# W3's last 64 features by tokens, W4 of tiles 0 to 2 with its output turned

## The chip, the core and the metric

The kernel runs on one core of one Trainium2 chip. Its engines run side by side, each with its own queue in which work is done in order: TensorE (PE in the profile; its weight loads are listed as PEld), VectorE (DVE), ScalarE (ACT), GpSimd (POOL) and SyncE (SP), which here issues almost all DMAs. The metric is the device time of one execution in microseconds (us), the median of several runs.

## The reference

The input x has 2048 tokens of 640 features. The result is a gated sum of a linear attention block and an MLP block with shifts between tokens:

```python
g = _sigmoid((x * gate_w).sum(-1, keepdims=True))
a = _A_ref(x, A_wqkv, A_wo)                 # linear attention, 32 heads of 20
b = _B_ref(x, B_w1, B_w2, B_w3, B_w4)
return g * a + (1 - g) * b

# _B_ref
h = _gelu(_layernorm(x, axis=-1) @ w1)
hs = jnp.concatenate([g0, g1, g2, g3], axis=-1) @ w2     # g0..g3: quarters of h, shifted by 1, -1, 2, -2 tokens
x1 = x + hs
h2 = _gelu(_layernorm(x1, axis=-1) @ w3) @ w4            # w3: 640 x 1728, w4: 1728 x 640
return x1 + h2
```

The change concerns w3 and w4. The inner width 1728 is 13 blocks of 128 features and a rest of 64.

## The kernel before, in words

The tokens are handled in four tiles of 512 (`TS`), each of four chunks of 128 (`CPT`). A first part, up to line 425, loads everything, makes the keys, queries and the attention's small matrix, and W1 of tiles 0 and 1. The part that the change touches is the loop over tiles at the end (L599 to L616). The order of the work on every engine is the order in which the program is written out (`tc.manual_schedule()`); nothing reorders it.

For a tile `t` the loop runs seven W3 units (`w3_unit`, L474). A unit does two blocks of 128 features (the last one does one): the weights of W3 are the stationary operand, the tile's 512 normalized tokens `lnT` are moved through, and the result, features on partitions and tokens in columns, goes through a gelu on ScalarE (L485) into `h2`. Between the units stand chunks of other work. `w2_unit` (L429) makes `x1` for a later tile and its statistics on VectorE (L439, L293 to L295), `ln2_apply` (L449) normalizes it (L453) and has it turned by a DMA transpose on SP. Tile 0 does this for tile 1, and tile 1 for tiles 2 and 3 (`ahead`, L598), so unit 2 and unit 3 of tile 1 are each followed by two W2 chunks. `att_unit` (L462) computes the attention's output of one chunk of tile `t` and VectorE adds it, times the gate, into `x1` (L470); its four chunks follow units 2 to 5.

The last 64 features of W3 (`w3_rest`, L488) are computed for two tiles at a time: after tile 0's units for tiles 0 and 1, in tile 1's W4 for tiles 2 and 3. The weights have 64 columns, so the left and the right half of the array work at once on the two halves of the tokens.

W4 (`w4_tile`, L548) takes a chunk of 128 tokens of `h2` as the stationary operand and moves w4's 640 output features through, as 256 and 384 columns. The result has tokens on partitions and features in columns, like the output. A chunk's 13 blocks are summed in PSUM; the 64 features of the rest are added by `w4_rest` (L521), in which upper and lower half of the array's rows work at once for two chunks. VectorE then forms `omg * result + x1` for all 640 features (L532), where `omg` is 1 - g and `x1` has been scaled by `omg` on ScalarE (`x1_scale`, L457), and SP stores the chunk (L537). `scale_t` (L276) scales the queries of the next tile on VectorE.

PSUM is handed out in pairs of two banks, four pairs in all:

```python
ps = ctx.enter_context(tc.tile_pool(name="ps", bufs=4, space=PSUM))
def pair():
    return ps.tile([P, 2, 512], F32, name="pp")
```

A new pair waits for the readers of an earlier one. The output chunks have two buffers (`outp`), and `hx_p` has two buffers of 512 columns, used by W1's last block (L359).

Of the kernel before, what the change touches and what calls it, by code (L numbers as in the profile page):

```python
# [7 lines left out]
ACT = mybir.ActivationFunctionType  # L8
ALU = mybir.AluOpType
BF16 = mybir.dt.bfloat16  # L10
# [6 lines left out]
def kernel(  # L17
# [13 lines left out]
    nc = tc.nc  # L31
    P = 128
    S, D = A_x.shape[1], A_x.shape[2]
    F = B_w3.shape[1]
    H, Dh = 32, 20
    NCH = S // P
    TS = 512
    NT = S // TS
    CPT = TS // P
    DC = D // P  # L40
    HD = D // 2
    FF = F // P
    FR = F - FF * P
# [12 lines left out]
    out2 = out.rearrange("b s d -> (b s) d")  # L56
# [4 lines left out]
    const = ctx.enter_context(tc.tile_pool(name="const", bufs=1))  # L61
    small = ctx.enter_context(tc.tile_pool(name="small", bufs=4))
    work = ctx.enter_context(tc.tile_pool(name="work", bufs=4))
    hx_p = ctx.enter_context(tc.tile_pool(name="hx_p", bufs=2))
    outp = ctx.enter_context(tc.tile_pool(name="outp", bufs=2))
    lnx_p = ctx.enter_context(tc.tile_pool(name="lnx_p", bufs=3))
    ps = ctx.enter_context(tc.tile_pool(name="ps", bufs=4, space=PSUM))
# [3 lines left out]
    def pair():  # L71
        return ps.tile([P, 2, 512], F32, name="pp")
# [4 lines left out]
    pqT = const.tile([P, DC, S], BF16)  # L77
# [3 lines left out]
    w3_sb = const.tile([P, DC, F], BF16)  # L81
# [16 lines left out]
    omg = const.tile([P, NCH], F32)  # L98
# [133 lines left out]
    for c in range(2, NCH):  # L232
        pt = pair()
# [42 lines left out]
    def scale_t(t):  # L276
        sl = pqT[:, :, t * TS:(t + 1) * TS]
        nc.vector.tensor_tensor(sl, sl, rb[:, t:t + 1, :].broadcast_to([P, DC, TS]), op=ALU.mult)
# [130 lines left out]
    w4_sb = w4p.tile([P, FF + 1, D], BF16)  # L409
    h2x_p = ctx.enter_context(tc.tile_pool(name="h2x_p", bufs=2))  # L410
# [15 lines left out]
    st = {}  # L426
# [17 lines left out]
    def ln2_rstd(t, c0, c1):  # L444
        if c0 == 0:
            st[t]["rstd"] = small.tile([P, CPT], F32, name="rstd2")
        rsqrt(st[t]["rstd"][:, c0:c1], st[t]["mv"][:, c0:c1, 1])
# [9 lines left out]
    def x1_scale(t, cc):  # L457
        c = t * CPT + cc
        x1 = st[t]["x1"][cc]
        nc.scalar.activation(x1[:], x1[:], ACT.Copy, scale=omg[:, c:c + 1])  # L460

    def att_unit(t, cc):  # L462
        c = t * CPT + cc
        pt = pair()
        for hf in range(2):
            for j in range(DC):
                nc.tensor.matmul(pt[:, hf, 0:HD], lhsT=pqT[:, j, c * P:(c + 1) * P],  # L467
                                 rhs=m_sb[:, j, hf * HD:(hf + 1) * HD], start=(j == 0), stop=(j == DC - 1))
        x1 = st[t]["x1"][cc][:].rearrange("p (h e) -> p h e", h=2)
        nc.vector.scalar_tensor_tensor(x1, pt[:, :, 0:HD], gate[:, c:c + 1], x1, op0=ALU.mult, op1=ALU.add)  # L470

    LT = TS // 2

    def w3_unit(t, i):  # L474
        if i == 0:
            st[t]["h2"] = h2p.tile([P, FF * TS], BF16, name="h2")
        h2, lnT = st[t]["h2"], st[t]["lnT"]
        pt = pair()
        n = min(2, FF - 2 * i)
        for k in range(n):  # L480
            fc = 2 * i + k
            for dc in range(DC):
                nc.tensor.matmul(pt[:, k, :], lhsT=w3_sb[:, dc, fc * P:(fc + 1) * P], rhs=lnT[:, dc, :],  # L483
                                 start=(dc == 0), stop=(dc == DC - 1))
        nc.scalar.activation(h2[:, 2 * i * TS:(2 * i + n) * TS], pt[:].rearrange("p h e -> p (h e)")[:, 0:n * TS],  # L485
                             ACT.Gelu_apprx_tanh)

    def w3_rest(ts, dsts):  # L488
        for t, dst in zip(ts, dsts):
            for dc in range(DC):  # L490
                for v in range(2):
                    nc.tensor.matmul(dst[FR * v:FR * (v + 1), :], lhsT=w3_sb[:, dc, FF * P:F],  # L492
                                     rhs=st[t]["lnT"][:, dc, v * LT:(v + 1) * LT], start=(dc == 0), stop=(dc == DC - 1))
        for t, dst in zip(ts, dsts):
            st[t]["h2x"] = h2x_p.tile([P, LT], BF16, name="h2x")
            nc.scalar.activation(st[t]["h2x"][:], dst, ACT.Gelu_apprx_tanh)

    NW = D - TS

    def w4_tiles(t, ccs, pts):  # L500
        if t < NT - 1:
            for cc in ccs:
                pt = pair()
                pts[cc, 0], pts[cc, 1] = (pt[:, 0, TS - LT:TS], 0, LT), (pt[:, 1, 0:D - LT], LT, D)
                pts[cc, "rest"] = pt[:, 0, 0:LT]
                pts[cc] = pt[:].rearrange("p h e -> p (h e)")[:, TS - LT:TS - LT + D]
        else:
            for _ in range(3 if 0 in ccs else 1):
                pts["pairs"] = pts.get("pairs", []) + [pair()]
            homes = {0: (0, 1), 2: (1, 2)} if 0 in ccs else {1: (3, 3), 3: (2, 0)}  # L510
            for cc, (w, n) in homes.items():
                wide, narrow = pts["pairs"][w][:, 0, :], pts["pairs"][n][:, 1, 0:NW]
                pts[cc, 0], pts[cc, 1] = (narrow, 0, NW), (wide, NW, D)

    def w4_mm(t, cc, pts, hf, start):
        dst, a, b = pts[cc, hf]
        for fc in range(FF):
            nc.tensor.matmul(dst, lhsT=st[t]["h2"][:, fc * TS + cc * P:fc * TS + (cc + 1) * P],  # L518
                             rhs=w4_sb[:, fc, a:b], start=start and fc == 0, stop=not start and fc == FF - 1)

    def w4_rest(t, pts):  # L521
        for u in range(2):
            for hf in range(2):
                for v in range(2):
                    rows = slice(FR * v, FR * (v + 1))
                    dst, a, b = pts[u + 2 * v, hf]
                    nc.tensor.matmul(dst, lhsT=st[t]["h2x"][rows, u * P:(u + 1) * P],  # L527
                                     rhs=w4_sb[rows, FF, a:b], start=u == 1, stop=u == 0)

    def w4_stt(t, cc, oc, src, a, b):  # L530
        c = t * CPT + cc
        nc.vector.scalar_tensor_tensor(oc[:, a:b], src, omg[:, c:c + 1], st[t]["x1"][cc][:, a:b],  # L532
                                       op0=ALU.mult, op1=ALU.add)

    def w4_store(t, cc, oc, a, b):
        c = t * CPT + cc
        nc.sync.dma_start(out2[c * P:(c + 1) * P, a:b], oc[:, a:b])  # L537

    def w4_out(t, cc, pts):
        oc = outp.tile([P, D], BF16, name="oc")  # L540
        if t < NT - 1:
            w4_stt(t, cc, oc, pts[cc], 0, D)
        else:
            for hf in range(2):
                w4_stt(t, cc, oc, *pts[cc, hf])
        w4_store(t, cc, oc, 0, D)

    def w4_tile(t):  # L548
        last = t == NT - 1
        pts = {}  # L550
        if not last:
            scale_t(t + 1)
        w4_tiles(t, (0, 2), pts)
        for cc in (0, 2):
            if not last:
                x1_scale(t + 1, cc)
            for hf in (1, 0):
                w4_mm(t, cc, pts, hf, True)
        w4_tiles(t, (1, 3), pts)
        w4_rest(t, pts)  # L560
        if t == 1:
            w3_rest((2, 3), (pts[0, "rest"], pts[2, "rest"]))
        for cc in (0, 2):
            w4_out(t, cc, pts)
        ocs = {}
        for cc, hf in ((1, 1), (3, 1), (1, 0), (3, 0)) if last else ((1, 0), (1, 1), (3, 0), (3, 1)):
            if not last and hf == 0:
                x1_scale(t + 1, cc)
            w4_mm(t, cc, pts, hf, False)
            if last:  # L570
                if hf == 1:
                    ocs[cc] = outp.tile([P, D], BF16, name="oc")
                w4_stt(t, cc, ocs[cc], *pts[cc, hf])
                w4_store(t, cc, ocs[cc], *pts[cc, hf][1:])
            elif hf == 1:
                w4_out(t, cc, pts)

    for cc in range(CPT):
        w2_unit(0, cc)
# [18 lines left out]
    ahead = {0: ((1, 0),), 1: ((2, 0), (3, 2))}  # L598
    for t in range(NT):  # L599
        for i in range(NW3):  # L600
            w3_unit(t, i)
            for u, i0 in ahead.get(t, ()):
                if 0 <= i - i0 < CPT:
                    w2_unit(u, i - i0)
                    ln2_rstd(u, i - i0, i - i0 + 1)
                    if i > i0:
                        ln2_apply(u, i - i0 - 1)
            if 2 <= i < 2 + CPT:
                att_unit(t, i - 2)
            for u, i0 in ahead.get(t, ()):  # L610
                if i - i0 == CPT - 1:
                    ln2_apply(u, CPT - 1)
        if t == 0:
            pt = pair()
            w3_rest((0, 1), (pt[:, 0, 0:LT], pt[:, 1, 0:LT]))
        w4_tile(t)  # L616


# [28 lines left out]
```

## Time and profile before

| | |
|---|---|
| three runs | 263.14, 263.43, 264.2 us; median 263.43 |
| profiled execution: span, first to last instruction | 261.2 us; what lies around it in that execution isn't recorded, and the median is 2.2 us above the span |
| TensorE busy | 257.1 us, 98% |
| VectorE, ScalarE, GpSimd busy | 141.6, 83.4, 26.9 us |
| W4 stage of tile 0 (128.36 to 143.25 us) | 14.89 us, TensorE 14.89, VectorE 2.72, ScalarE 3.52 |
| W3 stage of tile 1 (143.25 to 173.58 us) | 30.33 us, TensorE 30.33, VectorE 21.61, ScalarE 6.14 |
| granted TensorE clock in both | 1.00 |

The span is cut into 40 slices on the page, and each engine's busy share is given for a slice. The chain of work that ended last is followed back from the end of the kernel; an engine that takes nearly all of it sets the time. A line like L483 names the line of the kernel that issued the instruction. "Idle before" is the time in which an engine stood still just before an instruction, with the work that ended it.

### The profile page before, as it was taken

To read this page: it belongs to the slowest core of one execution; us is meant where nothing else is said; L and a number is where in the kernel's file an instruction comes from. 1 tells how busy PE (TensorE), PEld (TensorE's weight loads), DVE (VectorE), ACT (ScalarE), POOL (GpSimd) and SP (SyncE) were. 2 spreads that over 40 slices of the span, in tenths; PEclk is the share of its full clock that TensorE was granted. 3 is DMA by queue.
4 is the path that set the end of the run, shared out by engine and by line. 5 is a ranking of instruction groups with operands and counts; after the bars stand their busy time and mean duration, and the time that the engine had idled before them with its cause. 6 is when DMAs were issued, how large, how long until landed. Compare 5 with 4: busy or idle time off the path is not lost.

```text
span 261.2 us, 4169 instructions
## 1 busy us (share of the span) xinstructions
PE 257.1 (98%) x1669; PEld 158.7 (61%) x1669; DVE 141.6 (54%) x276; ACT 83.4 (32%) x125; POOL 26.9 (10%) x82
## 2 busy tenths in 40 slices
PE   7999999999999999999999999999999999999995
PEld 3777555788754644565676566567745567455553
DVE  2688778899947884967312378970312223112132
ACT  2655554321165446531520311140233350142100
POOL 3000050012220140131000123310000000000000
PEclk9999999999999999999999999999999999999999
DMA  7999997016684826996002011321200001100011
GB/s 210 203 138 376 365 267 318 0 28 125 125 100 86 220 56 143 173 311 83 0 3 75 25 28 25 75 54 25 77 25 0 0 3 50 53 0 0 0 53 50
DMA packets 47281, 25.78 MB, mean 99 GB/s; under 512 B 35230, under 2 KB 46494, under 8 KB 47262
## 3 DMA queue, kind: packets, MB, share of 16 engines
q1 hardware_dynamic: 46820, 25.03, 39.4%
q10 hardware_dynamic: 442, 0.49, 0.5%
q8 instruction: 13, 0.21, 0.4%
q14 instruction: 6, 0.05, 0.1%
HBM read 13.03 MB, written 3.60 MB: 64 GB/s over the span
## 4 chain that ended last, share of the span: by engine, by line
PE 97%; DMA 2%; SPq 0%; DVE 0%; issue 0%
PE pp L518 22%; PE pp L483 21%; PE pp L319 8%; PE pp L436 8%; PE pp L467 8%; PE pp L353 8%; PE pp L242 8%; PE pp L187 8%; DMA wk_sb<-in_A_wqkv_dram 2%; PE pp L527 1%; PE pp L492 1%; PE pp L386 1%; PE pp L372 1%; PE pp L257 0%; SPq L120 0%; SPq L126 0%
## 5 line engine op out<-in xcount | busy, mean ns | idle before, releaser
L483 PE MATMUL pp<-lnxT,w_sb 128*128 128x512 bf16 x260 | 60.0, 379 | 0.0
L518 PE MATMUL pp<-w_sb,h 128*128 128x384 bf16 (+3 forms) x416 | 57.9, 299 | 0.0
L485 ACT ACTIVATE h<-pp 128x1024 bf16<-128x1024 f32 (+1 forms) x28 | 26.9, 962 | 94.3 <-PE pp L483 94.3
L518 PEld LDWEIGHTS <-h 128*128 128x128 bf16 x416 | 38.3, 98 | 19.4 <-issue 1.2
L483 PEld LDWEIGHTS <-w_sb 128*128 128x128 bf16 x260 | 25.4, 98 | 27.2
L532 DVE SCALAR_TENSOR_TENSOR oc<-pp,omg,x 128x640 bf16<-128x640 f32 (+2 forms) x20 | 14.4, 748 | 45.4 <-PE pp L527 21.2
L470 DVE SCALAR_TENSOR_TENSOR x<-pp,gate,x 128x640 f32<-128x640 f32 x16 | 14.1, 879 | 33.6 <-PE pp L467 33.6
L179 ACT ACTIVATE e<-pp 128x640 bf16<-128x640 f32 (+1 forms) x26 | 21.5, 827 | 9.6 <-PE pp L242 9.6
L467 PE MATMUL pp<-m_sb,pqT 128*128 128x320 bf16 x160 | 24.3, 299 | 0.0
L436 PE MATMUL pp<-w_sb,hsT 128*128 128x320 bf16 x160 | 23.5, 299 | 0.0
L187 PE MATMUL pp<-wk_sb,xT 128*128 128x320 bf16 (+1 forms) x160 | 22.4, 300 | 0.5 <-DVE xT L216 0.3
L319 PE MATMUL pp<-x_sb,pk 128*128 128x320 bf16 (+1 forms) x160 | 22.0, 300 | 0.0
L242 PE MATMUL pp<-xT,hsT 128*128 128x512 bf16 x100 | 21.7, 379 | 0.0
L319 PEld LDWEIGHTS <-pk 128*128 128x128 bf16 x160 | 18.8, 117 | 3.2
L436 PEld LDWEIGHTS <-hsT 128*128 128x128 bf16 x160 | 15.6, 98 | 7.7
L467 PEld LDWEIGHTS <-pqT 128*128 128x128 bf16 x160 | 15.7, 98 | 7.7
L187 PEld LDWEIGHTS <-xT 128*128 128x128 bf16 x160 | 15.5, 98 | 6.9 <-DVE xT L216 0.6
L289 POOL TENSOR_SCALAR rstd<-mv 128x1 f32<-128x1 f32 (+1 forms) x20 | 7.7, 385 | 115.3 <-DVE mv L295 115.3
L439 DVE TENSOR_TENSOR x<-pp,x_sb 128x640 f32<-128x640 f32 x16 | 13.1, 818 | 10.7 <-PE pp L436 10.6
L353 PE MATMUL pp<-lnxT,w_sb 128*128 128x512 bf16 x80 | 18.1, 379 | 0.0
L242 PEld LDWEIGHTS <-hsT 128*128 128x128 bf16 x100 | 11.8, 118 | 9.7
L181 DVE SCALAR_TENSOR_TENSOR pk<-pp,e 128x640 bf16<-128x640 f32 x16 | 13.2, 825 | 1.7
(73 smaller groups left out, 190.3 us busy)
## 6 DMA issues: line engine op xcount, KB each, us to landing
x_sb<-in_A_x_dram SPq DMA_DIRECT2D x1, 2240.0 KB
out_dram<-oc SPq DMA_DIRECT2D x14, 160.0 KB, 1.8
w_sb<-in_B_w_dram SPq DMA_DIRECT2D x1, 2160.0 KB
w_sb<-in_B_w_dram SPq DMA_DIRECT2D x1, 2080.0 KB, 12.2
wo_sb<-in_A_wo_dram SPq DMA_DIRECT2D x6, 160.0 KB, 7.5
m_dram<-x SPq DMA_DIRECT2D x3, 320.0 KB, 2.8
hsT<-in_A_wqkv_dram SPq DMA_DIRECT2D x1, 800.0 KB, 5.4
m_sb<-in_A_wqkv_dram SPq DMA_DIRECT2D x1, 800.0 KB
```

Of the source, the lines that this page charges most:

```text
L179: nc.scalar.activation(ev, src, ACT.Exp)
L187: nc.tensor.matmul(pt[:, hf, 0:n], lhsT=xT[:, dc, c * P:(c + 1) * P], rhs=wk_sb[:, dc, hf * HD:hf * HD + n], start=(dc == first), stop=(dc ...
L242: nc.tensor.matmul(pt[:, t % 2, :], lhsT=wq_sb[:, dc, :].rearrange("p (m j) -> p j m", j=DC)[:, j], rhs=xT[:, dc, t * TS:(t + 1) * TS], st ...
L319: nc.tensor.matmul(pt[:, hf, 0:HD + hf], lhsT=w, rhs=x_sb[:, c, hf * HD:(hf + 1) * HD + hf], start=(c == 0), stop=(c == NCH - 1))
L353: nc.tensor.matmul(pt[:, i, :], lhsT=w, rhs=lnxT[t][:, dc, :], start=(dc == 0), stop=(dc == DC - 1))
L436: nc.tensor.matmul(pt[:, hf, 0:HD], lhsT=hsT[:, fc, 2 + c * P:2 + (c + 1) * P], rhs=w2_sb[:, fc, hf * HD:(hf + 1) * HD], start=(fc == 0), ...
L467: nc.tensor.matmul(pt[:, hf, 0:HD], lhsT=pqT[:, j, c * P:(c + 1) * P], rhs=m_sb[:, j, hf * HD:(hf + 1) * HD], start=(j == 0), stop=(j == D ...
L470: nc.vector.scalar_tensor_tensor(x1, pt[:, :, 0:HD], gate[:, c:c + 1], x1, op0=ALU.mult, op1=ALU.add)
L483: nc.tensor.matmul(pt[:, k, :], lhsT=w3_sb[:, dc, fc * P:(fc + 1) * P], rhs=lnT[:, dc, :], start=(dc == 0), stop=(dc == DC - 1))
L485: nc.scalar.activation(h2[:, 2 * i * TS:(2 * i + n) * TS], pt[:].rearrange("p h e -> p (h e)")[:, 0:n * TS], ACT.Gelu_apprx_tanh)
L518: nc.tensor.matmul(dst, lhsT=st[t]["h2"][:, fc * TS + cc * P:fc * TS + (cc + 1) * P], rhs=w4_sb[:, fc, a:b], start=start and fc == 0, stop ...
L532: nc.vector.scalar_tensor_tensor(oc[:, a:b], src, omg[:, c:c + 1], st[t]["x1"][cc][:, a:b], op0=ALU.mult, op1=ALU.add)
```

## The change

W3's last 64 features are now computed tile by tile, inside the pair of `att_unit` of chunk 0: the stationary operand is a chunk of 128 normalized tokens in the full array, the moving operand W3's last 64 columns, five matmuls for each of four chunks. The results have tokens on partitions. Two gelus write them twice, side by side, into a buffer of `hx_p`, and a DMA transpose turns that into `h2x`, features on partitions, both halves of the partitions holding the same 64 features.

W4 of tiles 0 to 2 is turned round: w4 is the stationary operand and `h2` with its 512 tokens moves through, for five blocks of 128 output features. The first four blocks have a bank each, in two pairs; the fifth is cut into two halves of 256 tokens in the two banks of a third pair. The 64 features of the rest come first. After each block ScalarE copies it to a buffer of `hx_p` (now three buffers), and a DMA transpose turns it into `pqT`, whose columns of this tile are no longer needed. The output step, with `x1`, follows in the next tile before its W3 unit 2, from SBUF. The last tile's W4 is as before, written out in one function; its rest takes the columns of `h2x` of its own chunk.

```diff
-    hx_p = ctx.enter_context(tc.tile_pool(name="hx_p", bufs=2))
+    hx_p = ctx.enter_context(tc.tile_pool(name="hx_p", bufs=3))
...
     def att_unit(t, cc):
...
+        if cc == 0:
+            w3_rest_mm(t, pt)
+            w3_rest_evac(t, pt)
         x1 = st[t]["x1"][cc][:].rearrange("p (h e) -> p h e", h=2)
         nc.vector.scalar_tensor_tensor(x1, pt[:, :, 0:HD], gate[:, c:c + 1], x1, op0=ALU.mult, op1=ALU.add)
...
-    def w3_rest(ts, dsts):
...
+    def w3_rest_mm(t, pt):
+        for u in range(2):
+            for v in range(2):
+                cc = 2 * u + v
+                for dc in range(DC):
+                    nc.tensor.matmul(pt[:, u, HD + FR * v:HD + FR * (v + 1)], lhsT=st[t]["lnT"][:, dc, cc * P:(cc + 1) * P],
+                                     rhs=w3_sb[:, dc, FF * P:F], start=(dc == 0), stop=(dc == DC - 1))
+
+    def w3_rest_evac(t, pt):
+        hr = hx_p.tile([P, TS], BF16, name="hx")
+        for r in range(2):
+            nc.scalar.activation(hr[:].rearrange("p (u v r f) -> p u v r f", u=2, v=2, r=2)[:, :, :, r],
+                                 pt[:, :, HD:HD + 2 * FR].rearrange("p u (v f) -> p u v f", v=2), ACT.Gelu_apprx_tanh)
+        st[t]["h2x"] = h2x_p.tile([P, TS], BF16, name="h2x")
+        nc.sync.dma_start_transpose(st[t]["h2x"][:].rearrange("p (c s) -> p c s", c=CPT), hr[:])
...
+    def w4_turned(t):
+        scale_t(t + 1)
+        prs = [pair() for _ in range(3)]
+        bank = [prs[d // 2][:, d % 2, :] for d in range(DC)]
+        outs = [(d, bank[d], 0, TS) for d in range(CPT)]
+        outs += [(CPT, bank[CPT][:, 0:LT], 0, LT), (CPT, prs[2][:, 1, 0:LT], LT, TS)]
+        for n, (d, dst, a, b) in enumerate(outs):
+            rows = slice(FR * (n % 2), FR * (n % 2 + 1))
+            nc.tensor.matmul(dst, lhsT=w4_sb[rows, FF, d * P:(d + 1) * P], rhs=st[t]["h2x"][rows, a:b],
+                             start=True, stop=False)
+        for d in range(DC):
+            if d < CPT:
+                x1_scale(t + 1, d)
+            for fc in range(FF):
+                for e, dst, a, b in outs:
+                    if e == d:
+                        nc.tensor.matmul(dst, lhsT=w4_sb[:, fc, d * P:(d + 1) * P],
+                                         rhs=st[t]["h2"][:, fc * TS + a:fc * TS + b], start=False, stop=(fc == FF - 1))
+            hT = hx_p.tile([P, TS], BF16, name="hx")
+            if d < CPT:
+                nc.scalar.copy(hT[:], bank[d])
+            else:
+                nc.scalar.copy(hT[:].rearrange("p (v s) -> p v s", v=2), prs[2][:, :, 0:LT])
+            nc.sync.dma_start_transpose(pqT[:, d, t * TS:(t + 1) * TS].rearrange("p (c f) -> p c f", c=CPT), hT[:])
+
+    def w4_turned_out(t, cc):
+        c = t * CPT + cc
+        oc = outp.tile([P, D], BF16, name="oc")
+        o = t * TS + cc * P
+        nc.vector.scalar_tensor_tensor(oc[:].rearrange("p (d f) -> p d f", d=DC), pqT[:, :, o:o + P], omg[:, c:c + 1],
+                                       st[t]["x1"][cc][:].rearrange("p (d f) -> p d f", d=DC), op0=ALU.mult, op1=ALU.add)
+        nc.sync.dma_start(out2[c * P:(c + 1) * P, :], oc[:])
...
-    def w4_tile(t):
...
+    def w4_last(t):
...
     for t in range(NT):
         for i in range(NW3):
+            if t > 0 and i == 2:
+                for cc in range(CPT):
+                    w4_turned_out(t - 1, cc)
             w3_unit(t, i)
...
-        if t == 0:
-            pt = pair()
-            w3_rest((0, 1), (pt[:, 0, 0:LT], pt[:, 1, 0:LT]))
-        w4_tile(t)
+        if t < NT - 1:
+            w4_turned(t)
+        else:
+            w4_last(t)
```

In the changed file the gelus of the rest are line L502, the remainder matmuls of the turned W4 L517, its main matmuls L525, the copies L529 and L531, their transposes L532, and the output step L538.

More of the change, by code (lines that the diff above doesn't have):

```diff
@@ L486, in w3_unit @@
                              ACT.Gelu_apprx_tanh)
-    def w3_rest(ts, dsts):
[L489 to L496, printed above, removed]
@@ L498 @@
-    NW = D - TS
-    def w4_tiles(t, ccs, pts):
-        if t < NT - 1:
-            for cc in ccs:
-                pt = pair()
[L504 to L528, printed above, removed]
+    def w3_rest_mm(t, pt):
[5 more added lines that the diff above has]
+                                     rhs=w3_sb[:, dc, FF * P:F], start=(dc == 0), stop=(dc == DC - 1))
@@ L537, in w4_store, with place, mm @@
         nc.sync.dma_start(out2[c * P:(c + 1) * P, a:b], oc[:, a:b])
[L539 to L543, printed above, removed]
+    def w4_last(t):
+        pts, ocs = {}, {}
+        def place(pairs, homes):
+            for cc, (w, n) in homes.items():
+                pts[cc, 0], pts[cc, 1] = (pairs[n][:, 1, 0:NW], 0, NW), (pairs[w][:, 0, :], NW, D)
+        def mm(cc, hf, start):
+            dst, a, b = pts[cc, hf]
+            for fc in range(FF):
+                nc.tensor.matmul(dst, lhsT=st[t]["h2"][:, fc * TS + cc * P:fc * TS + (cc + 1) * P],
+                                 rhs=w4_sb[:, fc, a:b], start=start and fc == 0, stop=not start and fc == FF - 1)
+        prs = [pair() for _ in range(3)]
+        place(prs, {0: (0, 1), 2: (1, 2)})
+        for cc in (0, 2):
+            for hf in (1, 0):
+                mm(cc, hf, True)
+        prs.append(pair())
+        place(prs, {1: (3, 3), 3: (2, 0)})
+        for u in range(2):
+            for hf in range(2):
+                for v in range(2):
+                    rows = slice(FR * v, FR * (v + 1))
+                    dst, a, b = pts[u + 2 * v, hf]
+                    cc = u + 2 * v
+                    nc.tensor.matmul(dst, lhsT=st[t]["h2x"][rows, cc * P:(cc + 1) * P],
+                                     rhs=w4_sb[rows, FF, a:b], start=u == 1, stop=u == 0)
+        for cc in (0, 2):
+            oc = outp.tile([P, D], BF16, name="oc")
@@ L544, in w4_out @@
             for hf in range(2):
                 w4_stt(t, cc, oc, *pts[cc, hf])
-        w4_store(t, cc, oc, 0, D)
-    def w4_tile(t):
[L549 to L576, printed above, removed]
+            w4_store(t, cc, oc, 0, D)
@@ L578 @@
+        for cc, hf in ((1, 1), (3, 1), (1, 0), (3, 0)):
+            mm(cc, hf, False)
+            if hf == 1:
+                ocs[cc] = outp.tile([P, D], BF16, name="oc")
+            w4_stt(t, cc, ocs[cc], *pts[cc, hf])
+            w4_store(t, cc, ocs[cc], *pts[cc, hf][1:])
     for cc in range(CPT):
@@ L612 @@
                     ln2_apply(u, CPT - 1)
-        if t == 0:
-            pt = pair()
-            w3_rest((0, 1), (pt[:, 0, 0:LT], pt[:, 1, 0:LT]))
-        w4_tile(t)
+        if t < NT - 1:
+            w4_turned(t)
+        else:
+            w4_last(t)
 _INS = ['A_x', 'A_wqkv', 'A_wo', 'B_x', 'B_w1', 'B_w2', 'B_w3', 'B_w4', 'gate_w']
```

## The prediction

> **What bounds the kernel now.** I read the page's busy table and clock first, then the chain of work in order of time, then the timeline around the W4 stages, then the groups by form.
>
> ```profile
> span 261.2 us, 4169 instructions
> ...
> PE 257.1 (98%) x1669; PEld 158.7 (61%) x1669; DVE 141.6 (54%) x276; ACT 83.4 (32%) x125; POOL 26.9 (10%) x82
> ...
> PEclk9999999999999999999999999999999999999999
> ```
>
> TensorE is busy for 257.1 of 261.2 us at full granted clock, and the idle rest lies in the first 6 us. So the change can win only what it takes out of TensorE's stream, and every wait that it puts into that stream is paid in full. The chain gives the price of that stream; its columns are start, length, what:
>
> ```profile
> 76.25 1.45 PE pp L372 x30
> ...
> 126.13 1.08 PE pp L483 x5
> 127.21 1.21 PE pp L492 x20
> 128.42 7.17 PE pp L518 x52
> 135.59 0.65 PE pp L527 x8
> 136.24 7.17 PE pp L518 x52
> ...
> 243.65 7.06 PE pp L518 x52
> ```
>
> L483: 1.08/5 = 216 ns for 512 columns. In the trace's start-to-start times 384, 320, 256 and 128 columns take 163, 136, 109 and 56 ns: columns/2.4 plus about 2.6 ns, whatever the weights. L518 at 128.42 is 26 x 163 + 26 x 109 = 7.07 us plus one change of array mode: each step between full-array and half-array matmuls (L483 to L492, L492 to L518, L518 to L527 and back) costs 90 to 96 ns over the normal pitch.
>
> **TensorE's own work.** *W4 of tiles 0 to 2.* Removed per tile: 52 x 163 + 52 x 109 ns = 14.14 us. Added: for features 0 to 511 52 x 216 ns, for the last 128 features 26 x 109 ns (two halves of 256 tokens): 14.07 us. Three tiles: -0.21. The 64-row remainders stay paired: two pairs of 109 and two of 163 ns (0.54 us) become two of 216 and one of 109 (0.54). *W3's last 64 features.* Before, 40 matmuls in 20 pairs of 109 ns, 2.2 us. After, 4 tiles x 20 matmuls of 64 columns; the formula gives 29 ns each, 2.35 us, +0.15. Bounds: in L372 the 40-column matmuls, each with its own 128x128 weights, start 25 to 28 ns apart, those of 120 columns 52 ns; so 2.1 to 4.2 us, that is -0.1 to +2.0. I take 29, as the 25 ns row shows that loading weights is no floor near it. *Mode changes.* Before 4 in tile 0, 3 in tile 1, 2 each in tiles 2 and 3, 11; after 2 a tile, 8: -0.28. Together **-0.35 us**.
>
> **The wait that is added.** In the built program of the changed kernel the first matmul of output block d=1 waits for ScalarE's copy of block d=0 (L529), and that of d=3 for the copy of d=2. Blocks 0 and 1 are the two banks of one pair tile, as are 2 and 3; the wait goes by the pair. Block 4 has a pair of its own and does not wait. Since d=1 is the very next work in TensorE's queue, everything behind stands: two stalls a tile, six in all. The timeline has each part of one (start, length, engine, line; in brackets the idle time and its releaser):
>
> ```profile
> 125.97 1.24 PE L483 MATMUL pp<-lnxT,w_sb 128*128 128x512 bf16 x5
> 126.24 0.88 DVE L470 SCALAR_TENSOR_TENSOR x<-pp,gate,x 128x640 f32<-128x640 f32 x1 [2.63 <-PE pp L467]
> 127.14 1.28 PE L492 MATMUL pp<-lnxT,w_sb 128*64 128x256 bf16 x20
> 127.25 0.60 ACT L485 ACTIVATE h<-pp 128x512 bf16<-128x512 f32 x1 [1.41 <-PE pp L483]
> ```
>
> L483's last matmul is through at 127.05 (127.14 less the mode change) and ScalarE starts at 127.25: 0.20 us. The copy:
>
> ```profile
> L216 ACT CAST xT<-pp 128x384 bf16<-128x384 f32 x1 | 0.5, 479 | 2.4 <-DVE xT L216 2.4
> L321 ACT CAST gs<-pp 128x640 bf16<-128x640 f32 x5 | 3.5, 692 | 19.7 <-PE pp L319 14.4 <-DMA wk_sb<-gs 5.3
> ```
>
> 479 ns for 384 and 692 for 640 elements make 585 for 512. The release to TensorE: at the kernel's start VectorE's copy L216 ends at 4.43 us and L187 begins at 4.49, 0.06. So 0.20 + 0.59 + 0.05 = 0.84 us a stall, six times: **+5.05 us**. Bounds: 0.70 (0.15 + 0.50 + 0.05) to 0.95 (0.25 + 0.63 + 0.07): 4.2 to 5.7. Nothing hides it, because no other matmul stands between.
>
> The Trainium skill, PSUM — Partial Sum Buffer, section "PSUM bank collisions raise a hardware error", asks for guards by bank and 32-partition quadrant, not by address; two engines on different banks run clean. By that rule d=1 could start beside the copy and the six stalls would be nil; no row of this trace shows the case. I go by the built program's waits.
>
> **Tile 1, two smaller waits.** Its W4 needs three pairs at once where two sufficed. By the built program the third, asked for by the fifth remainder matmul, is freed by the gelu of the last W3 unit. That gelu ends 0.20 + 0.60 after the unit's last matmul, TensorE asks 0.09 + 2 x 0.216 = 0.52 after it: stall 0.80 + 0.06 - 0.52 = **0.34 us**. In tiles 0 and 2 the third pair is freed by the last attention sum (L470, 0.20 + 0.88 after its matmuls), and the 1.08 us of L483 x5 and those 0.52 lie between: no stall.
>
> The other is VectorE. The output step of tile 0 (four L538) moves from tile 0's W4 stage, where VectorE had 2.7 of 14.9 us to do, to unit 2 of tile 1, where it keeps pace only just:
>
> ```profile
> 154.00 0.82 DVE L439 TENSOR_TENSOR x<-pp,x_sb 128x640 f32<-128x640 f32 x1 [1.04 <-PE pp L436]
> ...
> 155.91 0.57 DVE L453 TENSOR_SCALAR ln<-x,mv,rstd 128x640 bf16<-128x640 f32 x1
> 156.39 0.82 DVE L439 TENSOR_TENSOR x<-pp,x_sb 128x640 f32<-128x640 f32 x1
> ```
>
> A W2 chunk costs 1.91 us and its L453 0.48. Counted from tile 1's first W3 matmul: VectorE is through with L453 of chunk (2,0) at 9.65. An L538 reads bf16 and f32 from SBUF; bounds are L453 (0.58) and the old L532 from PSUM (0.88), I take 0.75. The first two end at 11.15. The third needs one of two output buffers, so the first store's landing:
>
> ```profile
> lnxT<-ln SPq DMA_TRANSPOSE x32, 2.6
> out_dram<-oc SPq DMA_DIRECT2D x14, 160.0 KB, 1.8
> ```
>
> SP is issuing L453's transpose (1.20 us) until 11.0; store 1.8: landed at 12.8, the third ends at 13.6, the fourth, after the second store, at 14.3. Then chunk (2,2), its L453 and L439 of chunk (3,0) free that chunk's pair at 14.3 + 1.91 + 0.48 + 0.86 + 0.06 = 17.6. TensorE asks for this pair at 17.38 (four W3 units of 2.16, five W2 chunks and one attention chunk of 1.36, and 0.59 for the W3 remainder come before chunk (3,1)): **0.25 us**, bounds 0 (L538 at 0.58) to 0.8 (at 0.88 and landings 0.3 later). By the next free pairs VectorE has caught up.
>
> **Priced at nothing.** The 15 copies (8.9 us) and eight gelus of the W3 remainder sit in ScalarE, 32% busy; a copy starts at once because x1_scale (0.82) ends 2 us earlier. The 15 transposes take SP about 1 us each, one per 2.8 us. The last lands 0.2 + 0.6 + 2.6 = 3.4 us after the tile's W4; tile 1 wants it at 9.65. In tiles 2 and 3 the output step then runs 3.5 to 7.8, and the first attention sum, which also waits for the remainder's two gelus, is due at 9.4: 1.6 us of cover; beyond it a late transpose would hold VectorE and, one pair later, TensorE. Stores of tile 2 issue some 9 us before the end of W3 in tile 3. The last tile's W4 and the tail keep their order.
>
> Sum: -0.35 + 5.05 + 0.34 + 0.25 = +5.3 us. The profiled execution's span is 261.2; the median of the three runs, 263.43 (263.14 to 264.2), is 2.2 above it for what lies around the span. The sum changes the span only: 266.5, and **268.7 us** as a run, +2.0%.
>
> **Rivals.** *The pairs do not hold TensorE back* (the other side): d=1 starts beside the copy, or the copy is over sooner. Then -0.35 + 0.34 + 0.25 leaves 263.7, no change; faster than -0.5% would need the other two gone and more. For it speaks that the two banks are distinct; against it, the wait in the program. It decides where a stall is under 0.18 us (1.1/6), a fifth of the copy's own path. *The 64-column matmuls run at the pace of the 120-column ones*, 52 ns: +1.85, 270.5; against it the 25 ns row. *VectorE's backlog in tile 1 spreads*: store landings of 2.6 (as a transpose) and 0.88 for L538 put VectorE 1.4 us later, and TensorE waits at two or three pairs: +1.5, 270.2. *The clock falls in the gaps*: the first matmuls of the kernel, before it is warm, start 427 ns apart; were one block after each stall at that pace, 13 x 0.21 x 6 = 16 us, 285. Against it: the granted clock is 1.00 in every stage now, a stall is 0.84 us in 2.8 us of dense work. The Trainium skill, TensorE: Matmul & The Clock Gate, section "A second HAM failure mode: psum-queue depth-cycling", reports that brief idling between matmul groups made the clock swing between half and full; that speaks against this change, and by it the 285 would be the better guess. No row of this trace has such gaps after warm-up.
>
> **How the numbers follow.** As forecast 0.73, no hold by pairs 0.06, slow 64-column matmuls 0.07, wider backlog 0.10, clock 0.04. A run-to-run spread of some 0.5% (1.3 us) is what can be told from no change. Faster 0.02, same 0.05, slower 0.93. The forecast's own bounds: 4.2 - 0.45 + 0.2 = +4.0 to 5.7 + 0.34 + 0.8 - 0.3 = +6.5. The range takes in the two dearer cases and some of the milder side: 266.8 to 271.0.
>
> **What would show it.** Right: TensorE idle before L525 six times, about 0.85 us each, released by ScalarE's copy, the largest row of TensorE in the list of waits; about 5 us more TensorE idle time; the W3 remainder near 0.6 us a tile; in tile 1 a gap of 0.3 before a remainder matmul. Wrong: L525 dense across d=0 to d=1, or a granted clock under 1.00 in the W4 stages, or waits of TensorE for VectorE over 1 us.

## The result, and the profile after

The changed kernel takes 271.75 us (median of 6 runs, 271.06 to 274.2) against 263.28 us (262.97 to 265.57): a ratio of 1.0317, 95% interval 1.0273 to 1.0362. Forecast were 268.7 us and at most 271.0. So the direction was right, and the time lies above the range.

The profiled execution has a span of 269.93 us and a time of its own of 271.77. From the page of the changed kernel, the span, TensorE's and the other engines' busy time, and the granted clock by slices:

```profile
span 269.9 us, 4148 instructions
...
PE 258.4 (96%) x1625; PEld 151.3 (56%) x1625; DVE 141.1 (52%) x276; ACT 93.4 (35%) x144; POOL 27.3 (10%) x82
...
PEclk9999999999999999999999999999999999999999
```

TensorE is busy 1.3 us more, in a span 8.7 us longer: what was lost is TensorE standing still. Even the 1.3 is no work: ahead of a gap a 512-column matmul counts to its modelled end, 379 ns, and in a dense row only to the next start, 216, so some nine gaps add 0.16 each. The clock is as before. The list of waits of TensorE in the changed kernel (who waited for whom; total us, times, longest) holds most of that in four lines:

```profile
PE pp L525 <- ACT hx L529: 4.2, 6, 0.7
PE pp L436 <- DVE x L439: 1.5, 2, 0.9
PE pp L211 <- DMA x_sb<-in_A_x_dram: 1.4, 1, 1.4
PE pp L200 <- PEq L647: 0.8, 1, 0.8
```

The fourth was there before. Not in it are a wait of 0.31 us in tile 1 and a longer end of the kernel, which the table below has. The chain of work in order of time (start, length, what), through tile 0's W4, shows the shape of the first:

```profile
129.73 2.93 PE pp L525 x13
132.65 0.02 issue
132.68 0.59 ACT hx L529
133.27 0.04 issue
133.31 4.38 PE pp L525 x20
...
139.17 0.59 ACT hx L529
139.76 0.04 issue
139.80 5.80 PE pp L525 x39
```

TensorE stands for the copy's 0.59 us and the hand-over on both sides. The list of waits counts idle time by modelled ends (4.2 us for six); I measure a gap as the time from one matmul's start to the next one's, less the normal pitch of its columns (columns/2.4 plus 2.6 ns). By that the six are 837 to 881 ns each, 5.20 us together. With the same measure for everything else:

| where | forecast, us | profiled execution, us |
|---|---|---|
| six stalls inside L525 | +5.05 | +5.20 |
| tile 1, third pair (before L517) | +0.34 | +0.31 |
| tile 1, VectorE late (before L436, twice) | +0.25 | +1.80 |
| TensorE's own work and mode changes | -0.35 | -0.37 |
| start: the second load of x lands late | 0 | +1.28 |
| end: last VectorE instruction to the end of the span | 0 | +0.52 |
| sum | +5.3 | +8.74 |
| span after less span before | | 269.93 - 261.23 = +8.70 |

Three rows were missed: tile 1's VectorE, the start and the end. The timeline of the changed kernel in tile 1 holds the first (start, length, engine, line; in brackets the idle time and its releaser):

```profile
155.07 1.68 DVE L538 SCALAR_TENSOR_TENSOR oc<-pqT,omg,x 128x640 bf16<-128x640 bf16 x2
155.18 1.20 SPq L455 DMA_TRANSPOSE lnxT<-ln  x1
156.47 5.33 SPq L540 DMA_DIRECT2D out_dram<-oc  x4
...
159.77 1.68 DVE L538 SCALAR_TENSOR_TENSOR oc<-pqT,omg,x 128x640 bf16<-128x640 bf16 x2 [3.02 <-DMA out_dram<-oc]
161.37 0.81 DVE L439 TENSOR_TENSOR x<-pp,x_sb 128x640 f32<-128x640 f32 x1
...
162.23 1.52 PE L436 MATMUL pp<-w_sb,hsT 128*128 128x320 bf16 x10 [0.62 <-DVE x L439]
```

The first store is issued at 156.47, where it was forecast (11.03 us after tile 1's first W3 matmul, forecast 11.0). The third L538 needs its landing, and starts at 159.77: 3.3 us later, where 1.8 had been taken, while VectorE idles for 3.02 us.

### The profile page after: what moved, and what is told of

It reads as the page before. It is cut to its first block, busy times and chain, and to the rows that moved or that the text cites. A ratio compares the mean times of both kernels' runs of the same rounds, so it can differ in the third digit from the quotient of the medians.

```text
span 269.9 us, 4148 instructions
## 1 busy us (share of the span) xinstructions
PE 258.4 (96%) x1625; PEld 151.3 (56%) x1625; DVE 141.1 (52%) x276; ACT 93.4 (35%) x144; POOL 27.3 (10%) x82
## 4 chain that ended last, share of the span: by engine, by line
PE 87%; issue 3%; DMA 3%; DVE 3%; ACT 2%; SPq 0%; DVEq 0%
PE pp L486 19%; PE pp L525 14%; PE pp L319 8%; PE pp L353 8%; PE pp L242 8%; PE pp L187 8%; PE pp L467 8%; PE pp L436 7%; PE pp L561 5%; DMA wk_sb<-in_A_wqkv_dram 2%; ACT hx L529 1%; DMA out_dram<-oc 1%; DVE oc L538 1%; DVE x L439 1%; PE pp L496 1%
## 5 line engine op out<-in xcount | busy, mean ns | idle before, releaser
L525 PE MATMUL pp<-h,w_sb 128*128 128x512 bf16 (+1 forms) x234 | 43.7, 343 | 4.2 <-ACT hx L529 4.2
L486 PEld LDWEIGHTS <-w_sb 128*128 128x128 bf16 x260 | 25.2, 98 | 26.5
L525 PEld LDWEIGHTS <-w_sb 128*128 128x128 bf16 x234 | 22.6, 98 | 25.2 <-issue 6.5
L538 DVE SCALAR_TENSOR_TENSOR oc<-pqT,omg,x 128x640 bf16<-128x640 bf16 x12 | 10.2, 881 | 41.4 <-DMA pqT<-hx 35.9
L436 PE MATMUL pp<-w_sb,hsT 128*128 128x320 bf16 x160 | 23.7, 299 | 1.5 <-DVE x L439 1.5
L242 PE MATMUL pp<-xT,hsT 128*128 128x512 bf16 x100 | 21.7, 379 | 0.0
L436 PEld LDWEIGHTS <-hsT 128*128 128x128 bf16 x160 | 15.6, 98 | 9.5 <-issue 2.0
L242 PEld LDWEIGHTS <-hsT 128*128 128x128 bf16 x100 | 11.8, 118 | 9.7
L529 ACT CAST hx<-pp 128x512 bf16<-128x512 f32 x12 | 7.0, 585 | 25.8 <-issue 18.9
```

What stands on the lines that cost most here:

```text
L242: nc.tensor.matmul(pt[:, t % 2, :], lhsT=wq_sb[:, dc, :].rearrange("p (m j) -> p j m", j=DC)[:, j], rhs=xT[:, dc, t * TS:(t + 1) * TS], st ...
L436: nc.tensor.matmul(pt[:, hf, 0:HD], lhsT=hsT[:, fc, 2 + c * P:2 + (c + 1) * P], rhs=w2_sb[:, fc, hf * HD:(hf + 1) * HD], start=(fc == 0), ...
L525: nc.tensor.matmul(dst, lhsT=w4_sb[:, fc, d * P:(d + 1) * P], rhs=st[t]["h2"][:, fc * TS + a:fc * TS + b], start=False, stop=(fc == FF - 1))
```

## The experiments

T below is tile 1's first W3 matmul, from which the prediction counted. The first four experiments ran on one chip, the last four on another; each time compares with runs of the kernel before on the same chip, taken alongside (263.05 us in the first four experiments, 263.20 in the last four).

### e1_order: another order of the blocks

```
-        for d in range(DC):
+        for d in (0, 2, 1, 3, 4):
```

> The turned W4 takes its output blocks in the order 0, 2, 1, 3, 4 instead of 0 to 4; nothing else is touched, every copy, wait and byte stays. Theory (TensorE is held because two blocks that follow each other lie in one pair, and the wait goes by the pair): block 2 lies in the other pair and starts beside the copy of block 0; block 1 waits for a copy that was over 2 us earlier. The six gaps before L525 (837 to 881 ns each, 5.2 us together) go, and the time falls from 271.75 to 266.5 us; ScalarE's copies run beside matmuls. Rival (a copy out of PSUM and a matmul into PSUM get in each other's way whatever the bank, so the time is lost in any order): gaps or slower matmuls of the same sum remain, 271.7.

Measured: 265.95 us (265.63 to 266.42, 8 runs), ratio 1.0100, interval 1.0073 to 1.0126. The list of waits of TensorE in this kernel:

```profile
PE pp L436 <- DVE x L439: 2.3, 2, 1.4
PE pp L200 <- PEq L647: 0.8, 1, 0.8
```

All six stalls are gone, though every copy is still made, and still takes 585 ns. In this order a block's pair has been drained while a block of the other pair runs. So the price of the stalls was the order of two banks of one pair tile, not ScalarE's work; the rival, that a copy and a matmul hinder each other whatever the bank, falls. The wait for VectorE in tile 1 did not stay as it was: 2.60 us by the measure of the table, 0.79 more than in the changed kernel. The time is nevertheless 0.55 us under the 266.5 expected: in this profile the first query matmul (L242) starts at 27.32 us, 1.27 earlier than in the changed kernel's.

### e2_outbufs: a third output buffer

```
-    outp = ctx.enter_context(tc.tile_pool(name="outp", bufs=2))
+    outp = ctx.enter_context(tc.tile_pool(name="outp", bufs=3))
```

> Three output buffers instead of two. Theory (in tile 1 the third output step waits until the first store has landed, 3.3 us after its issue because a transpose was issued just ahead of it, and VectorE's work behind it comes late): the third step no longer waits, the fourth waits for the same landing, so VectorE is 0.84 us (one step) earlier. Of the two gaps of TensorE in tile 1 (782 and 1019 ns) the first closes and the second stays near 0.96 us: -0.84 us, 270.9. Rival (VectorE has simply too much to do there, buffers do not matter): both gaps stay, 271.7.

Measured: 270.18 us (269.82 to 271.54, 4 runs), ratio 1.0262, interval 1.0209 to 1.0314. The two gaps of tile 1 fell from 1.80 to 1.41 us only, less than half of the fall expected; the rest of the gain is again an early start (L242 at 27.40 us, not 28.59). The third L538 no longer waits, but the fourth does. The timeline of this kernel:

```profile
153.98 1.20 SPq L455 DMA_TRANSPOSE lnxT<-ln  x1
155.27 4.94 SPq L540 DMA_DIRECT2D out_dram<-oc  x4
158.97 0.88 DVE L538 SCALAR_TENSOR_TENSOR oc<-pqT,omg,x 128x640 bf16<-128x640 bf16 x1 [2.63 <-DMA out_dram<-oc]
```

The landing of the first store is late whichever step asks for it. SP's third store took 1.60 us to issue in place of 0.33.

### e4_early: the output step one unit earlier

```
-            if t > 0 and i == 2:
+            if t > 0 and i == 1:
```

> The four output steps of the tile before stand ahead of W3 unit 1 instead of unit 2; two buffers as before. VectorE's work is the same, but no transpose is issued just ahead of the stores, and VectorE has 1.6 us of idle time there. Theory: stores land in about 1.9 us, the fourth step ends about 10.1 us after tile 1's first W3 matmul instead of 15.9, both gaps in tile 1 go: -1.8 us, 269.95. Rival (too much work for VectorE in tile 1): the backlog is the same one unit earlier, gaps of 1 us or more remain in tile 1, 271 to 271.8.

Measured: 268.74 us (268.67 to 268.84, 4 runs), ratio 1.0198, interval 1.0153 to 1.0243. Its list of waits of TensorE:

```profile
PE pp L525 <- ACT hx L529: 4.2, 6, 0.7
PE pp L200 <- PEq L647: 0.8, 1, 0.8
```

Both gaps behind VectorE are gone, and the six stalls are as they were: they do not hang on the gaps. The same store is issued at T + 6.62 with no transpose ahead of it, and the step that needs its landing starts 1.9 us later. (Nor does an instruction packet pass there, which matters below: so this run alone does not say which of the two was in the way.) The time fell 1.2 us further than expected; the first query matmul (L242) starts at 27.44 us here and at 28.59 in the changed kernel's profile, 1.15 later, which is nearly all of that.

### e0_before: the kernel before, once more

> The kernel before once more, unchanged, for its profile. In the changed kernel's profile the second load of x came 1.3 us later than in the one profile of before, and the end after the last store took 0.5 us longer; 1.8 of the 8.7 us between the two spans. Theory (these vary from execution to execution): the start of the query stage (L242), 27.3 us in the one profile and 28.6 in the other, differs between executions of one kernel by up to about 1 us. Rival (the change does it, by way of the program's size or layout): L242 starts at 27.3 again here, and at 28.6 in every version of the changed kernel.

Measured: 264.0 us (one run), span 262.30, L242 at 28.38 against 27.31 in the first profile of the same kernel. So a start about 1.1 us later occurs in the kernel before as well, with no instruction changed. In the other experiments, with and without the change, L242 starts between 27.3 and 27.9 us. The end did not vary: 2.32 us from the last VectorE instruction to the end of the span, as in the first profile.

### What was in the store's way

The landings of the first store differed in ways that neither the transpose nor the order of the stores explains: 3.30, 4.09 and, in e2_outbufs, 3.70 us. The packets in the window from the first store's issue to the third L538, in the changed kernel, show more. The digits are the busy share of the 16 DMA engines in 40 slices, then what they moved:

```profile
DMA  9999999951009567989889896211000000000000
GB/s 215 212 218 209 227 209 218 197 103 31 0 0 293 109 233 280 389 311 389 281 311 373 311 389 249 47 16 16 0 16 16 16 31 16 31 16 31 16 0 0
...
q1 hardware_dynamic: 910, 0.48, 52.6%
q8 instruction: 1, 0.02, 2.0%
```

The first block of busy slices is the transpose, the second the stores, at some 350 GB/s. From the 26th slice to the 38th nearly nothing moves: 16 GB/s is a single packet of 1,280 bytes in a slice of 82 ns, so one engine working alone. I take it for the queue of one engine, which is through 1 us after the others. In the same window one packet of 16 KB passes on the queue q8, named instruction; it starts at 157.46 and takes 1.07 us. Thirteen such packets pass in the span, some 20 us apart, 0.21 MB in all: over TensorE's 1,625 matmuls and as many weight loads that is 64 bytes each. The Trainium skill, Runtime: NRT & Kernel Launch, section "Instruction fetch mechanics", says that an engine's program is refilled in blocks of 16 KiB, 256 instructions, by a DMA queue of its own, and that the cost of crossing a block is mostly hidden. The size and the number agree with the trace. No row of the waits shows TensorE waiting for a block; the question was whether a store does.

In five executions the packet, the landing and the gaps, in us after T:

| kernel | store issued | code packet | next L538 needing a landing | fourth L538 | gaps of tile 1 |
|---|---|---|---|---|---|
| changed | 11.03 | 12.02 to 13.09 | 14.33 | 15.13 | 1.80 |
| e8_after_again | 11.03 | 12.17 to 13.55 | 14.81 | 15.61 | 2.29 |
| e1_order | 11.03 | 12.78 to 13.74 | 15.12 | 15.92 | 2.60 |
| e2_outbufs | 11.03 | 12.09 to 13.46 | 14.73 | 14.73 | 1.41 |
| e7_code_shift | 11.03 | 8.73 to 9.66 | 13.17 | 13.97 | 0.64 |

The landing follows the packet's end by 1.2 to 1.4 us in the first four rows, and the gaps are the fourth L538's start less 13.32 in all five, to 0.01.

The profiles hold the same thing at another place, the store of tile 1's last output chunk, some 57 us after T. In the changed kernel, e8_after_again, e1_order, e4_early and e5_order_early a code packet is on its way when SP issues that store. The issue takes 0.41, 0.95, 0.80, 0.97 and 0.46 us, and each time it is over 0.36 to 0.44 us after the packet's end. In e2_outbufs and e7_code_shift no packet passes during the issue, and it takes 0.33. Not every issue is held up: in e1_order and e5_order_early a store of the last tile was issued beside a packet in 0.33 us.

### e7_code_shift: the code packet moved

```
     def q_unit(j, i):
         pt = pair()
+        if (j, i) == (0, 0):
+            warmup(24, 16, pt)
```

> The changed kernel with 24 matmuls of 16 columns more, once, ahead of the first q unit, far from tile 1 (they write a PSUM region that the q unit then starts afresh, so nothing of the result changes). In the trace a packet of 16 KB on queue q8 (instruction) starts 12.0 us after tile 1's first W3 matmul, takes 1.07 us, and some ten packets of the first output store are through only when it is over. The 24 matmuls are 48 more TensorE instructions of the about 256 between two such packets, so that packet should come about 4 us sooner. Theory that this packet delays the store's landing: third L538 starts 12.7 to 12.9 us after tile 1's first W3 matmul instead of 14.3, TensorE's two gaps in tile 1 fall from 1.80 to 0.2 to 0.4 us; the median is that of the changed kernel -1.5 + 0.7 for the 24 matmuls. Rival that a store behind a transpose on SP's queue lands late for itself: third L538 at 14.3, gaps 1.80, the median +0.7.

Measured: 270.98 us (270.59 to 271.24, 4 runs), ratio 1.0293, interval 1.0279 to 1.0307. The same window, in this kernel:

```profile
DMA  9999999999841000194889999899999994000000
GB/s 218 206 222 214 218 218 206 214 227 210 173 85 34 4 0 0 21 189 105 294 315 357 357 357 399 315 337 336 357 357 378 357 420 127 0 0 0 0 0 0
...
q1 hardware_dynamic: 903, 0.48, 70.5%
```

No code packet, and no tail of one engine. From its timeline:

```profile
155.15 1.68 DVE L540 SCALAR_TENSOR_TENSOR oc<-pqT,omg,x 128x640 bf16<-128x640 bf16 x2
155.26 1.20 SPq L457 DMA_TRANSPOSE lnxT<-ln  x1
156.56 4.18 SPq L542 DMA_DIRECT2D out_dram<-oc  x4
158.69 1.68 DVE L540 SCALAR_TENSOR_TENSOR oc<-pqT,omg,x 128x640 bf16<-128x640 bf16 x2 [1.87 <-DMA out_dram<-oc]
```

With the transpose still right ahead of the store, the wait for the landing is 2.13 us from the issue, not 3.3 to 3.8, and of the two gaps one is gone and the other is 0.64 us. So the code packet, not the transpose, was the larger part; the rival falls. My own figures were somewhat low: 13.17 for the third L538 where I had said 12.7 to 12.9, and 0.64 us of gap where I had said 0.2 to 0.4.

The median fell by 0.55 us against the changed kernel measured alongside (e8_after_again), not by the 0.8 expected, and its list of waits of TensorE says why:

```profile
PE pp L527 <- ACT hx L531: 4.2, 6, 0.7
PE pp L200 <- PEq L649: 0.8, 1, 0.8
PE pp L374 <- DMA wk_sb<-gs: 0.6, 1, 0.6
PE pp L438 <- DVE x L441: 0.5, 1, 0.5
```

The third line is new (lines are two higher in this kernel). The 24 matmuls moved every later code packet, and another of them now starts at 71.04 us, among the transposes of gs: ScalarE's second L321 waits 6.08 us for them, against 5.28 in e8_after_again, and TensorE loses 0.80 us by the start-to-start measure. The spans add up: -1.64 in tile 1, +0.80 here, +0.15 at the start (the 24 matmuls and the loads of x) make -0.69; 268.87 - 269.54 is -0.67.

### e8_after_again: the changed kernel, once more

> The changed kernel as it is, once more. The kernel before started 1.1 us later in one profiled execution than in another, at the second load of x. If the late start of the first profiled execution of the changed kernel belonged to that execution: 270.5 us, first k matmul of the third chunk at 27.3 us. If it belongs to the changed program: 271.7, at 28.6.

Measured: 271.53 us (270.94 to 273.34, 4 runs), ratio 1.0333, interval 1.0297 to 1.0369; profiled span 269.54. The expectation of 270.5 was wrong, and so was its alternative: L242 (the first query matmul; the expectation calls it a k matmul) starts at 27.73, so most of the late start was indeed of one execution, but the code packet came later and longer, and the gaps of tile 1 were 2.29 us in place of 1.80:

```profile
PE pp L525 <- ACT hx L529: 4.2, 6, 0.7
PE pp L436 <- DVE x L439: 2.0, 2, 1.1
PE pp L200 <- PEq L647: 0.8, 1, 0.8
```

What the start gave back, tile 1 took. How much tile 1 loses is thus not a fixed number of this kernel.

### e5_order_early: both waits taken out

```
-        for d in range(DC):
+        for d in (0, 2, 1, 3, 4):
...
-            if t > 0 and i == 2:
+            if t > 0 and i == 1:
```

> W4's turned blocks in the order 0, 2, 1, 3, 4 and the output step at unit 1 instead of unit 2. If the two groups of waits are separate sums, both go: no TensorE gap inside L525, none before chunks (2,2) and (3,0) of tile 1; left are -0.37 of TensorE's own work, +0.31 for the third pair of tile 1 and +0.52 at the kernel's end. From 263.05 that is 263.5 us: no difference from the kernel before that can be told. If the reordered blocks make a new wait (all copies then crowd at the end of the stage, the transposes land later and the output step at unit 1 waits for them): 264.5 or more, with TensorE waiting for VectorE in tile 1 or 3.

Measured: 263.76 us (263.27 to 264.88, 11 runs), ratio 1.0021, interval 1.0010 to 1.0031. Its list of waits of TensorE:

```profile
PE pp L200 <- PEq L647: 0.8, 1, 0.8
PE pp L211 <- DMA x_sb<-in_A_x_dram: 0.3, 1, 0.3
```

Two edits of one line each take back 7.8 of the 8.3 us between e8_after_again and the kernel before. What is left, +0.56 us in the medians, is as expected: -0.37 of TensorE's own work, +0.31 for tile 1's third pair, +0.52 at the end make +0.46. No new wait came.

### e6_w3_only: W3's last 64 features alone

W4 and its output are those of the kernel before; only the rest of W3 is made as in the changed kernel. Its core:

```
+        if cc == 0:
+            w3_rest_mm(t, pt)
+            w3_rest_evac(t, pt)
...
-                    nc.tensor.matmul(dst, lhsT=st[t]["h2x"][rows, u * P:(u + 1) * P],
+                    nc.tensor.matmul(dst, lhsT=st[t]["h2x"][rows, (u + 2 * v) * P:(u + 2 * v + 1) * P],
...
-        if t == 0:
-            pt = pair()
-            w3_rest((0, 1), (pt[:, 0, 0:LT], pt[:, 1, 0:LT]))
```

> One part alone: W3's last 64 features by tokens in the full array and turned by DMA; W4 as before. 20 pairs of 109 ns become 80 matmuls of 29 ns, +0.15 us; mode changes 11 to 8, -0.28; nothing else on TensorE's path: 262.9 us, no difference that can be told, and no wait of TensorE for VectorE or ScalarE. If this part carries a loss of its own (the gelus or the transpose of the remainder late for W4): above 264.

Measured: 263.28 us (262.85 to 263.85, 11 runs), ratio 1.0003, interval 0.9995 to 1.0012. No wait of TensorE beyond the one at the start of every kernel. This half of the change costs nothing and gains nothing that can be measured. Its end takes 0.28 us longer than that of the kernel before, and that is about what its mode changes save.

No kernel here is faster than the one before.

## Why the prediction was right or wrong

**The six stalls: right.** Forecast 0.84 us each from 0.20, 0.59 and 0.05; measured 0.837 to 0.881. The copy is 585 ns, the interpolation's number. e1_order shows the mechanism: with the pairs alternating, no stall. That weighs against the rival that the pairs do not hold TensorE back. It says nothing on what the banks themselves would allow, since every kernel here keeps the program's wait; the rule weighed in the prediction (guards by bank) is neither shown nor refuted.

**Own work, mode changes, third pair: right.** The 64-column matmuls start 29.1 ns apart (29 forecast), so the rival of 52 ns is out. Mode changes cost 92 to 103 ns. TensorE's own work came to -0.37 (-0.35), the third pair to 0.31 (0.34).

**The clock: right.** The granted clock is 1.00 in the changed kernel, with gaps of 0.84 us in every W4 stage. The prediction had priced the swinging clock that the Trainium skill, TensorE: Matmul & The Clock Gate, section "A second HAM failure mode: psum-queue depth-cycling", reports for brief idling between matmul groups at some 285 us. The runs decide against it for gaps of this length and number.

**Tile 1's VectorE: the step that failed.** The place, the order and the arithmetic held: L453 ends at T + 9.71 (forecast 9.65), the store issues at T + 11.03 (11.0), L538 comes every 0.80 us (0.75), and the loss follows from the fourth L538. What failed is one term, "store 1.8: landed at 12.8". The row that gave it says x14, but that counts issues: the trace of the kernel before has a landing for only two of those fourteen stores (1.80 and 1.78 us), both in a stretch with no packets but those of stores. Here the wait from the issue to the step that needs the landing was 3.30 to 4.09 us, as a code packet of 0.96 to 1.38 us lay on one engine's queue among the store's packets. With the packet moved away it was 2.13, and the gap 0.64 us, inside the forecast's bounds of 0 to 0.8; the bound "landings 0.3 later" was the right one for the store and the transpose, and had no term for a third party. The prediction's own sign of being wrong, waits of TensorE for VectorE over 1 us, is in the list of waits: 1.5. The rival "VectorE's backlog in tile 1 spreads" had about the right price, 1.5 us more, for a reason of its own (landings of 2.6 us as a transpose) that e7_code_shift does not bear out. Its 270.2 fell short by the next two terms.

**Start and end: not priced.** The forecast's sum had no term for either. (What lies around the span was 1.84 us in the profiled execution, against the 2.2 taken: that made up 0.36. The 2.2 set the median of three runs against the span of an execution whose own time is not on record; where both are known for one run of the kernel before, it is 1.7 to 1.8.) The prediction also put all of TensorE's idle time into the first 6 us. Of those 4.1 us 2.7 lie behind the last matmul, which ends at 258.53, so that the end of the kernel had a price to watch. The start varies from one execution to the next, by 1.1 us in the kernel before itself, so it is no part of the change; of the 1.28 us in the first profile 0.86 were gone in e8_after_again. The end is a part of it: 2.83 to 2.84 us in every version with the turned W4, 2.32 in both profiles of the kernel before. From the last store's issue to the end of SP's wait for that landing it is 1.5 us in both; the closing instructions after it take 1.31 us in place of 0.80. In the kernel before SP's waits on other queues lie ahead of that last landing, in the changed one they come after it, four of about 0.07 us; that is 0.28, and e6_w3_only, with the same order, ends 0.28 later. For the remaining 0.2 no run here gives a reason.

**The verdict.** Slower, at a chance of 0.93, was right. The range's upper end was 0.75 us too low. Taking the code packet's part out of tile 1 (1.80 - 0.64 = 1.16) would have put 271.75 at about 270.6, inside it. In that execution the late start alone, 0.86 us against e8_after_again, would have done as much; but in e8_after_again, which started early, tile 1 lost 2.29 us and the median is still 271.53.

## What to carry to other kernels

Where the end of a block and the start of the next use two halves of one tile, walk the halves of different tiles in turn: here that took back 5.2 us with one line. A step that waits for a landing and sits where its engine only just keeps pace should be placed where it has slack of more than the median landing, since here a late landing, not the median one, set what was lost; one unit earlier cost nothing and took back 1.8 to 2.3 us. Before a landing is priced, look at which instruction packets cross that window, and take both cases into the range.

## What was not expected of the hardware

A 16 KB instruction packet, by its number and by e7_code_shift one of TensorE's, passes about every 20 us, and it can hold up other transfers. In these runs one packet put 1.2 to 2.0 us on a 160 KB store's landing (2.13 us without it, 3.30 to 4.09 with it), 1.3 us on the issue of a store behind it in SP's queue (1.60 against 0.33 us), and 0.8 us on the transposes of gs that TensorE waited for. So 24 added matmuls of some 25 ns, 118 us ahead of tile 1, changed a wait in tile 1 by 1.64 us, and made another of 0.80 that ends at 77.5 us: the position of a stretch in TensorE's program is a hidden variable of its DMA timing. It varies between executions too, as the packet's start and length do (0.96 to 1.38 us beside the store in tile 1). The changed kernel's ten runs lie between 270.94 and 274.2, and the four of e4_early, whose steps are out of the packet's way, between 268.67 and 268.84. That the packet makes this difference in spread is not shown: the kernel before, which has no such wait, has runs from 262.82 to 265.57. That the packet and the late queue share one engine is inferred from the tail at a single engine's rate and from e7_code_shift; the trace does not number the engines.
